# A cross-stage rework of a fused attention and MLP block's schedule: split first load, trickled weight loads, interleaved attention chain

## The chip, the cores and the metric

The kernel runs on one core of one Trainium2 chip. The metric is the device time of one execution in microseconds (us). The kernel before took 895.39 us (median of 4 runs, 894.59 to 896.08). All runs used below are fast unless the text says otherwise.

Ratios are the mean time of one kernel's fast runs over the mean of the fast runs of the kernel before in the same rounds, so they are not quite the ratio of the quoted medians. The kernel before drifted between calls (medians 895.07 to 897.00), so runs of different calls are compared by their ratios.

TensorE is called PE below, VectorE DVE, ScalarE ACT, and the engine that issues the loads SP. A bank is one of the eight parts of `ps`, into which PE writes its results; an eviction is the instruction by which DVE or ACT takes them out. Half clock is a stretch in which the granted clock of PE is 0.5, or, where no clock is recorded, its instructions take about twice their usual time.

## The reference

```python
# S=2048 rows, D=1024, 32 heads of 32, F=3584, bf16
def A(x):                                  # linear attention, x already layernormed
    q, k, v = split(x @ wqkv)              # D -> 3D
    phi = lambda t: where(t > 0, t + 1, exp(t)) + 1e-6
    kv = einsum("bhsd,bhse->bhde", phi(k), v);   z = phi(k).sum over s
    num = phi(q) @ kv;   den = phi(q) @ z + 1e-6
    return (num / den) @ wo
def B(x):                                  # gated MLP
    return (relu(x @ W_gate) * (x @ W_up)) @ W_down
h  = x + A(layernorm(x))
h2 = h + B(layernorm(h))
```

## The kernel before

Rows go in 16 tiles of 128, four of them to a row block of 512. Every instruction is recorded in program order per engine; a small planner turns reads and writes of named buffers (`_Buf`) into semaphore waits. Each engine runs its own list in order. One queue (SP) issues all loads and stores.

The pieces, by the names of the program: `ln1`, `T1` (layernorm and transposes of an x tile), `kvp` (k and v of a tile, 32 matmuls), `kvacc` (adds to kv and z), `kvfin` (masked kv and z to SBUF as `kvm` and `zc`), `a1` (one q unit: 8 matmuls for 128 columns of q over a row block), `a2` (numerator and denominator), `a3` (transposes of o), `a4` (output projection, h, layernorm of h), `a5` (transposes of the normalized h), `g_unit` (gate and up), `d_round` (down).

```python
# loads, in the order in which SP issues them
load_x1(0); load_wkv(0); load_x1(1)
for nt in range(1, NKV): load_wkv(nt)            # 4 chunks of 1 MB in all
for st in range(2, NX1): load_x1(st)             # NX1 = 4 slots for x tiles
for i in range(ND2): load_wq(i)                  # 2 x 1 MB
for i in range(ND2): load_wo(i)                  # 2 x 1 MB
for _ in range(NGS): load_g_next()               # 4 x 1 MB of gate and up weights

ln1(0); ln1(1); T1(0)
for st in range(NST):                            # ln1(st) also issues load_x1(st + 4)
    if st + 1 < NST: T1(st + 1)
    if st + 2 < NST: ln1(st + 2)
    kvp(st)
    if st >= 1: kvacc(st - 1)
kvacc(NST - 1); kvfin()
# ... x2 and W_down loads ...
for (sb_, ct) in a1_units[:26]: a1(sb_, ct, ALL)        # 26 of 32 q units first
for j in range(STB): a2(0, j, ALL)
for j in range(STB):
    if j == STB - 1: filler(ALL)                        # a filler is one of the other 6 q units
    a3(0, j, ALL)
# then a4(0) a4(1) a4(2) a5(0) a4(3) a5(1) f f a5(2) f f a5(3) f
# ...
def a4(r, j, pool):
    ...                                                  # 2 x 8 matmuls, h = . + x
    layernorm(hsb[:, hs, j, :], B_h[hs][j], xn[:, st % 2, :], B_xn[st % 2], "dve", ...)
def a5(r, j, pool):
    (b,) = alloc_banks(pool)
    transpose8(xn[:, st % 2, :], [B_xn[st % 2]], b, NDC, ...)
    ...
# last: d_round: all matmuls of four banks, then four evictions (DVE) and four stores
```

Of the kernel before, what the change touches and what calls it, by code (L numbers as in the profile page):

```python
# [45 lines left out]
class _Plan:  # L46
# [48 lines left out]
    def emit(self, e, eng):  # L95
        seen = {}
        for op in self.prog[e]:
# [15 lines left out]
            ins = op.fn(eng)  # L113
            if last is not None:
                ins._wait_ge(last[0], last[1])
# [6 lines left out]
def bass_sequential_preLN__linear_attn_block__glu_gated_reglu__prompt_kernel(  # L122
# [51 lines left out]
    with es:  # L174
# [89 lines left out]
        sl_x1 = slots("dx1_", NX1)  # L264
        sl_wkv = slots("dwkv_", NKV)
# [11 lines left out]
        B_x1 = bufs("x1_", NX1)  # L277
# [9 lines left out]
        B_kvm = _Buf("kvm")  # L287
        B_zsb = _Buf("zsb")
        B_zc = _Buf("zc")
# [80 lines left out]
        def load_x1(st):  # L370
            i = st % NX1
            dma_load(sl_x1[i], x1[:, i, :], xv[st * P:(st + 1) * P, :], [B_x1[i]], "ld_x1_%d" % st)
# [141 lines left out]
        def ln1(st):  # L514
            i = st % NX1
            layernorm(x1[:, i, :], [B_x1[i]] * NBC, xn[:, st % 2, :], B_xn[st % 2], "dve", "ln1_%d" % st)
            if st + NX1 < NST:
                load_x1(st + NX1)
# [39 lines left out]
        def kvfin():  # L558
            for g in range(NG):
# [3 lines left out]
                       reads=[B_bank[kb], B_bmask], writes=[B_kvm], name="kvm_%d" % g)  # L563
            PL.add("dve", lambda e: e.tensor_copy(out=zsb[:], in_=ps[:, BZ, 0:NG]),
                   reads=[B_bank[BZ]], writes=[B_zsb], name="zsb")
            for g in range(NG):
                PL.add("dve", lambda e, g=g: e.tensor_scalar(out=zc[:, g, :], in0=bmask4[:], scalar1=zsb[:, g:g + 1],
                                                             scalar2=None, op0=ALU.mult),
                       reads=[B_zsb, B_bmask4], writes=[B_zc], name="zc_%d" % g)
# [12 lines left out]
        def a2(r, j, pool):  # L582
# [6 lines left out]
            for g in range(NG):  # L589
# [3 lines left out]
                   True, True, [B_pqT[r][g], B_kvm], B_bank[nbk], "num_%d_%d" % (st, g))  # L593
                mm(ps[:, db, g * HPG:(g + 1) * HPG], pqT[:, r, g, j * P:(j + 1) * P], zc[:, g, :],
                   True, True, [B_pqT[r][g], B_zc], B_bank[db], "den_%d_%d" % (st, g))
# [76 lines left out]
        def d_round(r, dh, banks4):  # L672
# [3 lines left out]
            for ft in range(NFT):  # L676
                c, fl = ft // FTB, ft % FTB
                ws = wd_slot(r, dh, c)
                for j in range(STB):
                    mm(bank(banks4[j], NW), hhT[:, ft, j * P:(j + 1) * P], wdring[:, ws, fl, :],  # L680
                       ft == 0, ft == NFT - 1, [B_hhT[ft], B_wd[ws]], B_bank[banks4[j]],
                       "d_%d_%d_%d" % (r, dh, ft))
                if fl == FTB - 1:
                    load_wd_next()
            for j in range(STB):
# [12 lines left out]
        load_x1(0)  # L698
# [5 lines left out]
        for st in range(2, min(NX1, NST)):  # L704
            load_x1(st)
        for i in range(ND2):
            load_wq(i)
        for i in range(ND2):
            load_wo(i)
        for _ in range(NGS):  # L710
            load_g_next()
# [5 lines left out]
        for st in range(NST):  # L717
            if st + 1 < NST:
                T1(st + 1)
            if st + 2 < NST:  # L720
                ln1(st + 2)
            kvp(st)
# [4 lines left out]

        load_x2(0)
        if NST > 1:
            load_x2(1)  # L730
        for _ in range(NWS):
            load_wd_next()

        ALL = list(range(8))
        a1_units = [(sb_, ct) for sb_ in range(NSB) for ct in range(NG)]
        HB = min(6, max(0, len(a1_units) - NG))
        fillers = a1_units[len(a1_units) - HB:] if HB else []
        for (sb_, ct) in a1_units[:len(a1_units) - HB]:
            a1(sb_, ct, ALL)

        def filler(pool):
            if fillers:
                sb_, ct = fillers.pop(0)
                a1(sb_, ct, pool)

        for j in range(STB):
            a2(0, j, ALL)
        for j in range(STB):
            if j == STB - 1:
                filler(ALL)  # L750
            a3(0, j, ALL)
        seq = []
        for j in range(STB):
            seq.append(("a4", j))
            if j >= 2:
                seq.append(("a5", j - 2))
        for j in range(max(0, STB - 2), STB):
            seq.append(("f", 0))
            seq.append(("f", 0))
            seq.append(("a5", j))  # L760
        seq.append(("f", 0))
        for kind, j in seq:
            if kind == "a4":
                a4(0, j, ALL)
            elif kind == "a5":
                a5(0, j, ALL)
            else:
                filler(ALL)
        while fillers:
            filler(ALL)  # L770
# [4 lines left out]
        for r in range(NSB):  # L775
            bgq = []
            if r + 1 < NSB:
                rn = r + 1
                order = []
                order += [("a2", 0), ("a2", 1), ("a2", 2), ("a3", 0), ("a2", 3), ("a3", 1), ("a4", 0),  # L780
                          ("a3", 2), ("a4", 1), ("a3", 3), ("a5", 0), ("a4", 2), ("a5", 1), ("a4", 3),
                          ("a5", 2), ("nop", 0), ("a5", 3)]
                order = [(k_, j) for (k_, j) in order if j < STB]
                for k_, j in order:
                    bgq.append((k_, rn, j))
            lastpair = None
            for ft in range(NFT):
# [3 lines left out]
                if bgq:  # L791
                    k_, rn, j = bgq.pop(0)
                    if k_ == "a2":
                        a2(rn, j, BG)
                    elif k_ == "a3":
                        a3(rn, j, BG)
                    elif k_ == "a4":
                        a4(rn, j, BG)
                    elif k_ == "a5":
                        a5(rn, j, BG)  # L800
            while bgq:
                k_, rn, j = bgq.pop(0)
                if k_ == "a2":
                    a2(rn, j, BG)
                elif k_ == "a3":
                    a3(rn, j, BG)
                elif k_ == "a4":
# [65 lines left out]
```

## Time and profile before

| what | us |
|---|---|
| span of the profiled run | 894.4 |
| PE busy | 849.3 (95%) |
| PE work in full flow, counted (below) | 844 |
| wait for the fifth x tile, PE | 10.37 |
| q and attention of row block 0 (155.2 to 249.9) | 94.7 |
| end of the last matmul to the end of the span | 4.2 |

The busy table and the rows of 40 slices of the page; a digit is tenths of the slice, PEclk the granted PE clock:

```profile
PE 849.3 (95%) x4521; PEld 409.5 (46%) x4608; DVE 276.4 (31%) x517; ACT 174.4 (20%) x258; POOL 35.1 (4%) x107
PE   5689999997699999999999999999999999999998
PEclk9989999999799999999999999999999999999999
DMA  9911400000014435554244455543235653553052
```

The three weak places of the PE row are the start, the second slice (up to about 45 us) and slices 10 and 11. The rest is full. How full is told by counting: in full flow a 128x512 matmul starts every 0.2158 us. The Trainium skill, "TensorE: Matmul & The Clock Gate", section "Wait — 56ns, not 53.3ns?", gives 215.7 ns, and this trace agrees. The kernel has 3,712 of those, 384 transposes (0.058 us each), 128 k/v plus z pairs (0.080) and 128 numerator plus denominator pairs (0.083): 844 us.

The windows view of the kernel before cuts the span into stages (us of the window, then busy us and number of instructions per engine, the clock, the DMA share and GB/s):

```profile
core 0: us, PE busy (x) PEld busy (x) DVE busy (x) ACT busy (x) POOL busy (x), PEclk, DMA share, GB/s
11.60:36.97 25.37, 24.20 (x143) 11.81 (x143) 7.55 (x16) 9.99 (x15) 2.12 (x6) 1.00 1.10 351
36.97:57.77 20.80, 10.20 (x64) 5.21 (x64) 9.14 (x19) 3.65 (x6) 2.85 (x8) 0.75 0.45 145
155.24:249.93 94.69, 80.76 (x440) 39.93 (x448) 53.16 (x115) 26.15 (x39) 4.24 (x12) 0.93 0.04 12
249.93:890.17 640.24, 636.78 (x3202) 300.17 (x3263) 156.39 (x263) 92.15 (x137) 12.71 (x36) 1.00 0.44 138
```

The MLP (last line, with the attention of blocks 1 to 3 inside) takes what its instructions need. From 11.60 to 36.97 us the DMA is busy throughout: share 1.10, 351 GB/s. The Trainium skill, "DMA: Bandwidth & Descriptors", section "Specifications", gives a limit of about 358 GB/s per core. The rate here is close to it, but it is no hard limit in this case: e8, a run below, moved 370 GB/s from 4 to 8 us. The stretch 36.97 to 57.77 lasts 20.8 us, and its PE work is one step of 8.0 us. Why it takes longer is in the timeline, here of SP (issue of loads; a merged line covers the time from the first of its loads to the last) and then of DVE and PE:

```profile
31.28 2.92 SPq L368 DMA_DIRECT2D gring<-in_B_W_up_dram  x1
34.31 24.86 SPq L368 DMA_DIRECT2D RE<-in_A_x_dram  x7
...
43.99 1.29 DVE L465 BATCH_NORM_STATS2 st<-RE 128x6 f32<-128x512 bf16 x2 [16.43 <-DMA RE<-in_A_x_dram]
47.58 1.01 PE L445 MATMUL ps<-ident,xn 128*128 128x128 bf16 x8 [10.37 <-DVE xn L485]
48.82 8.32 PE L435 MATMUL ps<-RB,RA 128*128 128x512 bf16 x31 [0.23 <-DVE E2t L497]
```

The bracket at the end is the idle time ahead of the instruction and what ended it. The fifth x tile was issued only at 34.31, behind 8 MB of weights that nobody needs before 155 us, and reached DVE at 43.99. PE waited 10.37 us, and then 32 matmuls took 8.3 us instead of 6.9: half clock. The Trainium skill, "TensorE: Matmul & The Clock Gate", section "What's actually happening", says that the clock halves after an idle window of about 3.4 us and comes back after as much work. This trace agrees here: its clock records give half clock from 41.54 to 51.78 us.

Row block 0's layernorms (DVE, writing `xn`) and what PE does around them, from the timeline:

```profile
217.78 0.55 DVE L485 TENSOR_SCALAR xn<-hsb,rstd,nmr 128x1024 bf16<-128x1024 bf16 x1 [1.37 <-POOL nmr L476]
222.32 0.55 DVE L485 TENSOR_SCALAR xn<-hsb,rstd,nmr 128x1024 bf16<-128x1024 bf16 x1 [1.36 <-POOL nmr L476]
226.87 0.55 DVE L485 TENSOR_SCALAR xn<-hsb,rstd,nmr 128x1024 bf16<-128x1024 bf16 x1 [1.37 <-POOL nmr L476]
227.56 1.01 PE L445 MATMUL ps<-ident,xn 128*128 128x128 bf16 x8 [6.40 <-DVE xn L485]
238.25 0.62 PE L445 MATMUL ps<-ident,xn 128*128 128x128 bf16 x8 [4.13 <-DVE xn L485]
249.93 3.62 PE L435 MATMUL ps<-RE,gring 128*128 128x512 bf16 x16
```

PE waits 6.40 and 4.13 us for a layernorm. The last line is the first gate matmul.

The tail, from the timeline: one merged PE line that ends at 890.17, the four evictions, the four stores.

```profile
874.68 15.49 PE L435 MATMUL ps<-wdring,RA 128*128 128x512 bf16 x70
889.62 2.48 DVE L689 TENSOR_TENSOR RC<-ps,hsb 128x512 bf16<-128x512 f32 x4 [21.69 <-PE ps L435]
890.34 2.12 SPq L694 DMA_DIRECT2D out_dram<-RC  x4
```

### The profile page before, as it was taken

To read this page: it belongs to the slowest core of one execution; us is meant where nothing else is said; L and a number is where in the kernel's file an instruction comes from. 1 tells how busy PE (TensorE), PEld (TensorE's weight loads), DVE (VectorE), ACT (ScalarE), POOL (GpSimd) and SP (SyncE) were. 2 spreads that over 40 slices of the span, in tenths; PEclk is the share of its full clock that TensorE was granted. 3 is DMA by queue.
4 is the path that set the end of the run, shared out by engine and by line. 5 is a ranking of instruction groups with operands and counts; after the bars stand their busy time and mean duration, and the time that the engine had idled before them with its cause. 6 is when DMAs were issued, how large, how long until landed. Compare 5 with 4: busy or idle time off the path is not lost.

```text
span 894.4 us, 10887 instructions
## 1 busy us (share of the span) xinstructions
PE 849.3 (95%) x4521; PEld 409.5 (46%) x4608; DVE 276.4 (31%) x517; ACT 174.4 (20%) x258; POOL 35.1 (4%) x107
## 2 busy tenths in 40 slices
PE   5689999997699999999999999999999999999998
PEld 2345555444254444444544444454444444444443
DVE  3155443657343422013434111054321012121111
ACT  3234443331122221000222210022221001111100
POOL 1011110000000000000000000000000000000000
PEclk9989999999799999999999999999999999999999
DMA  9911400000014435554244455543235653553052
GB/s 318 338 37 36 143 1 1 1 1 24 24 42 148 130 107 169 183 165 142 95 137 133 155 172 178 168 142 118 95 119 163 189 187 114 169 164 119 24 175 84
DMA packets 105392, 109.75 MB, mean 123 GB/s; under 512 B 2944, under 2 KB 101248, under 8 KB 105344
## 3 DMA queue, kind: packets, MB, share of 16 engines
q1 hardware_dynamic: 105344, 109.06, 38.5%
q8 instruction: 36, 0.59, 0.3%
q14 instruction: 12, 0.10, 0.0%
HBM read 104.86 MB, written 4.19 MB: 122 GB/s over the span
## 4 chain that ended last, share of the span: by engine, by line
PE 87%; DVE 5%; SPq 4%; ACT 2%; issue 1%; DMA 1%; POOL 1%; DVEq 0%; ACTq 0%
PE ps L435 84%; SPq L368 4%; PE ps L445 3%; DVE RB L500 2%; ACT Et L495 2%; DMA RE<-in_A_x_dram 1%; DVE E2t L497 1%; DVE st L465 1%; DVE hsb L631 0%; POOL rstd L473 0%; DVE RE L606 0%; DVE xn L485 0%; POOL nmr L476 0%; DVE RC L689 0%; DVE kvm L561 0%
## 5 line engine op out<-in xcount | busy, mean ns | idle before, releaser
L435 PE MATMUL ps<-RE,gring 128*128 128x512 bf16 x876 | 196.7, 379 | 1.1
L435 PE MATMUL ps<-RC,gring 128*128 128x512 bf16 x877 | 194.8, 379 | 1.1
L435 PE MATMUL ps<-wdring,RA 128*128 128x512 bf16 x878 | 193.1, 379 | 0.9
L663 DVE TENSOR_TENSOR RA<-RC,ps 128x512 bf16<-128x512 bf16 x112 | 76.9, 687 | 262.1 <-PE ps L435 262.1
L661 ACT ACTIVATE RC<-ps 128x512 bf16<-128x512 f32 x112 | 67.0, 598 | 461.8 <-PE ps L435 461.8
L435 PEld LDWEIGHTS ps<-wdring,RA 128*128 128x128 bf16 x896 | 87.7, 98 | 105.7
L435 PEld LDWEIGHTS ps<-RC,gring 128*128 128x128 bf16 x896 | 87.1, 98 | 102.9
L435 PEld LDWEIGHTS ps<-RE,gring 128*128 128x128 bf16 x896 | 86.3, 98 | 100.1
L435 PE MATMUL ps<-RB,RA 128*128 128x512 bf16 x497 | 112.8, 386 | 1.4 <-DVE E2t L497 0.7
L435 PEld LDWEIGHTS ps<-RB,RA 128*128 128x128 bf16 x512 | 50.1, 99 | 59.4 <-issue 3.9
L689 DVE TENSOR_TENSOR RC<-ps,hsb 128x512 bf16<-128x512 f32 x32 | 19.9, 683 | 178.3 <-PE ps L435 178.3
L435 PE MATMUL ps<-wo,RE 128*128 128x512 bf16 x249 | 59.3, 389 | 0.4
L435 PE MATMUL ps<-RA,RC 128*128 128x512 bf16 x248 | 57.0, 387 | 2.0 <-DVE kvm L561 1.3
L495 ACT ACTIVATE Et<-ps 128x512 bf16<-128x512 f32 x64 | 38.2, 597 | 73.3 <-PE ps L435 30.4
L445 PE MATMUL ps<-ident,xn 128*128 128x128 bf16 x256 | 21.1, 230 | 31.4 <-DVE xn L485 30.7
L435 PEld LDWEIGHTS ps<-wo,RE 128*128 128x128 bf16 x256 | 25.6, 100 | 31.3 <-issue 2.7
L435 PEld LDWEIGHTS ps<-RA,RC 128*128 128x128 bf16 x256 | 25.3, 100 | 31.7 <-issue 2.8
L497 DVE TENSOR_SCALAR E2t<-Et 128x512 bf16<-128x512 bf16 x64 | 18.7, 293 | 65.7 <-ACT Et L495 65.6
L453 ACT ACTIVATE RE<-ps 128x1024 bf16<-128x1024 bf16 x24 | 24.3, 1023 | 56.2 <-PE ps L445 56.2
L445 PEld LDWEIGHTS ps<-ident,xn 128*128 128x128 bf16 x256 | 16.9, 103 | 36.4 <-issue 17.3
L631 DVE TENSOR_TENSOR hsb<-ps,x 128x512 bf16<-128x512 f32 x32 | 21.9, 690 | 32.5 <-PE ps L435 32.5
L470 POOL TENSOR_SCALAR ve<-mv 128x1 f32<-128x1 f32 x32 | 7.1, 223 | 609.4 <-DVE mv L468 609.4
(45 smaller groups left out, 328.9 us busy)
## 6 DMA issues: line engine op xcount, KB each, us to landing
gring<-in_B_W_gate_dram SPq DMA_DIRECT2D x28, 1024.0 KB, 5.3
gring<-in_B_W_up_dram SPq DMA_DIRECT2D x28, 1024.0 KB, 7.3
wdring<-in_B_W_down_dram SPq DMA_DIRECT2D x56, 512.0 KB, 3.6
RE<-in_A_x_dram SPq DMA_DIRECT2D x16, 256.0 KB, 2.8
RB<-in_A_wqkv_dram SPq DMA_DIRECT2D x4, 1024.0 KB, 9.2
x<-in_A_x_dram SPq DMA_DIRECT2D x16, 256.0 KB, 2.6
out_dram<-RC SPq DMA_DIRECT2D x32, 128.0 KB, 3.6
RC<-in_A_wqkv_dram SPq DMA_DIRECT2D x2, 1024.0 KB, 11.2
```

Source lines behind the costliest of these rows:

```text
L368: return PL.add("sp", lambda e: e.dma_start(dst_ap, src_ap), writes=wbufs, slot=slot, name=name)
L435: lambda e: e.matmul(out_ap, lhsT, rhs, start=start, stop=stop, skip_group_check=skip),
L445: lambda e, i=i: e.transpose(tb[:, i, :], src_ap[:, i * P:(i + 1) * P], ident[:]),
L453: PL.add("act", lambda e: e.activation(out=dst_ap, in_=src, func=ACTF.Identity), reads=[B_bank[b]], writes=dst_bufs, name=name)
L465: PL.add("dve", lambda e, c=c: e.bn_stats(out=st6[:, k, c * 6:(c + 1) * 6], in_=src_full[:, c * BCH:(c + 1) * BCH]), reads=[src_chunk_bufs ...
L495: PL.add("act", lambda e: e.activation(out=Et[:, k, 0:w], in_=src, func=ACTF.Exp), reads=[B_bank[b]], writes=[B_E[k]], name=name + "_exp")
L497: PL.add("dve", lambda e: e.tensor_scalar(out=E2t[:, k, 0:w], in0=Et[:, k, 0:w], scalar1=1.0, scalar2=1e-6, op0=ALU.min, op1=ALU.add), rea ...
L500: PL.add("dve", lambda e: e.scalar_tensor_tensor(out=dst_ap, in0=src, scalar=C1, in1=E2t[:, k, 0:w], op0=ALU.add, op1=ALU.max), reads=[B_b ...
L631: PL.add("dve", lambda e, b=b, nt=nt: e.tensor_tensor(out=hsb[:, hs, j, nt * NW:(nt + 1) * NW], in0=bank(b, NW), in1=x2[:, xs, nt * NW:(nt ...
L661: PL.add("act", lambda e: e.activation(out=rg[:, k, :], in_=bank(ga, SBW), func=ACTF.Relu), reads=[B_bank[ga]], writes=[B_rg[k]], name="rg ...
L663: PL.add("dve", lambda e: e.tensor_tensor(out=hhT[:, ft, :], in0=rg[:, k, :], in1=bank(gb, SBW), op=ALU.mult), reads=[B_rg[k], B_bank[gb]] ...
L689: PL.add("dve", lambda e, j=j, k=k: e.tensor_tensor(out=outst[:, k, :], in0=bank(banks4[j], NW), in1=hsb[:, hs, j, dh * NW:(dh + 1) * NW], ...
```

## The change

It keeps every computation and moves them: the first x tile is loaded in two halves; bulk weights are issued a few at a time during the k/v stage; the attention chain of row block 0 starts after its own 8 q units, with the other 24 spread between its pieces; the last output round evicts each bank while the next one's last matmuls run; `kvm` and `zc` get one dependency record per group. (It also attaches names to instructions, which adds none.)

```diff
-        B_kvm = _Buf("kvm")
+        B_kvm = bufs("kvm_", NG)            # the same for zc
...
-        load_x1(0)
+        load_x1(0, split=True)              # two loads of 128 KB on two semaphores
...
-        for i in range(ND2): load_wq(i)     # and wo, gate/up, x2, W_down: all at once
+        bulk = [...]                        # wq, wo, x2(0), x2(1), 4 gate/up, 4 W_down
+        def trickle(n): ...                 # issues the next n of them
...
                 ln1(st + 2)
+            if st >= 1:
+                trickle(2)
             kvp(st)
...
-        # 26 q units, then a2 x4, a3 x4, a4/a5 with 6 fillers (as above)
+        for ct in range(NG):
+            a1(0, ct, ALL)
+        chain = [("a2", 0), ("a2", 1), ("a2", 2), ("a3", 0), ("a2", 3), ("a3", 1), ("a4", 0),
+                 ("a3", 2), ("a4", 1), ("a3", 3), ("a5", 0), ("a4", 2), ("a5", 1), ("a4", 3),
+                 ("a5", 2), ("a5", 3)]
+        # behind each piece: 2 q units (first 8 pieces) or 1 (last 8), from blocks 1 to 3
...
+                if stagger and c == nchunks - 1:     # last round, last 4 of 28 weight tiles
+                    for j in range(STB):
+                        for ft in fts:
+                            d_mm(ft, j)
+                        d_evac(j)
```

More of the change, by code (lines that the diff above doesn't have):

```diff
@@ L113, in emit @@
             ins = op.fn(eng)
+            if op.name:
+                try:
+                    ins.annotate(op.name)
+                except Exception:
+                    pass
             if last is not None:
@@ L264, in bass_sequential_preLN__linear_attn_block__glu_gated_reglu__prompt_kernel @@
         sl_x1 = slots("dx1_", NX1)
+        sl_x1h = slots("dx1h_", NBC)
         sl_wkv = slots("dwkv_", NKV)
@@ L276, in bass_sequential_preLN__linear_attn_block__glu_gated_reglu__prompt_kernel @@
         B_bank = bufs("bank", 8)
-        B_x1 = bufs("x1_", NX1)
+        B_x1 = [bufs("x1_%d_" % i, NBC) for i in range(NX1)]
         B_xn = bufs("xn_", 2)
@@ L286, in bass_sequential_preLN__linear_attn_block__glu_gated_reglu__prompt_kernel @@
         B_E2 = bufs("E2_", 3)
-        B_kvm = _Buf("kvm")
+        B_kvm = bufs("kvm_", NG)
         B_zsb = _Buf("zsb")
-        B_zc = _Buf("zc")
+        B_zc = bufs("zc_", NG)
         B_pqT = [bufs("pqT%d_" % r, NG) for r in range(NSB)]
@@ L368, in dma_load, with load_x1 @@
             return PL.add("sp", lambda e: e.dma_start(dst_ap, src_ap), writes=wbufs, slot=slot, name=name)
-        def load_x1(st):
+        def load_x1(st, split=False):
             i = st % NX1
-            dma_load(sl_x1[i], x1[:, i, :], xv[st * P:(st + 1) * P, :], [B_x1[i]], "ld_x1_%d" % st)
+            if split and NBC > 1:
+                for c in range(NBC):
+                    dma_load(sl_x1h[c], x1[:, i, c * BCH:(c + 1) * BCH], xv[st * P:(st + 1) * P, c * BCH:(c + 1) * BCH],
+                             [B_x1[i][c]], "ld_x1_%d_%d" % (st, c))
+            else:
+                dma_load(sl_x1[i], x1[:, i, :], xv[st * P:(st + 1) * P, :], B_x1[i], "ld_x1_%d" % st)
         def load_wkv(nt):
@@ L515, in ln1 @@
             i = st % NX1
-            layernorm(x1[:, i, :], [B_x1[i]] * NBC, xn[:, st % 2, :], B_xn[st % 2], "dve", "ln1_%d" % st)
+            layernorm(x1[:, i, :], B_x1[i], xn[:, st % 2, :], B_xn[st % 2], "dve", "ln1_%d" % st)
             if st + NX1 < NST:
@@ L562, in kvfin @@
                                                              op=ALU.mult),
-                       reads=[B_bank[kb], B_bmask], writes=[B_kvm], name="kvm_%d" % g)
+                       reads=[B_bank[kb], B_bmask], writes=[B_kvm[g]], name="kvm_%d" % g)
             PL.add("dve", lambda e: e.tensor_copy(out=zsb[:], in_=ps[:, BZ, 0:NG]),
@@ L568, in kvfin @@
                                                              scalar2=None, op0=ALU.mult),
-                       reads=[B_zsb, B_bmask4], writes=[B_zc], name="zc_%d" % g)
+                       reads=[B_zsb, B_bmask4], writes=[B_zc[g]], name="zc_%d" % g)
         def a1(sb_, ct, pool):
@@ L592, in a2 @@
                 mm(ps[:, nbk, (col % 512):(col % 512) + P], pqT[:, r, g, j * P:(j + 1) * P], kvm[:, g, :],
-                   True, True, [B_pqT[r][g], B_kvm], B_bank[nbk], "num_%d_%d" % (st, g))
+                   True, True, [B_pqT[r][g], B_kvm[g]], B_bank[nbk], "num_%d_%d" % (st, g))
                 mm(ps[:, db, g * HPG:(g + 1) * HPG], pqT[:, r, g, j * P:(j + 1) * P], zc[:, g, :],
-                   True, True, [B_pqT[r][g], B_zc], B_bank[db], "den_%d_%d" % (st, g))
+                   True, True, [B_pqT[r][g], B_zc[g]], B_bank[db], "den_%d_%d" % (st, g))
             PL.add("dve", lambda e: e.tensor_scalar(out=dtmp[:, k, :], in0=ps[:, db, 0:H], scalar1=1e-6,
@@ L670, in bass_sequential_preLN__linear_attn_block__glu_gated_reglu__prompt_kernel, with d_round @@
         os_ctr = [0]
-        def d_round(r, dh, banks4):
+        def d_round(r, dh, banks4, stagger=False):
             hs = r % 2
@@ L675, in d_round, with d_mm, d_evac @@
                 touch_bank(b)
-            for ft in range(NFT):
+            def d_mm(ft, j):
                 c, fl = ft // FTB, ft % FTB
                 ws = wd_slot(r, dh, c)
-                for j in range(STB):
-                    mm(bank(banks4[j], NW), hhT[:, ft, j * P:(j + 1) * P], wdring[:, ws, fl, :],
-                       ft == 0, ft == NFT - 1, [B_hhT[ft], B_wd[ws]], B_bank[banks4[j]],
-                       "d_%d_%d_%d" % (r, dh, ft))
-                if fl == FTB - 1:
-                    load_wd_next()
-            for j in range(STB):
+                mm(bank(banks4[j], NW), hhT[:, ft, j * P:(j + 1) * P], wdring[:, ws, fl, :],
+                   ft == 0, ft == NFT - 1, [B_hhT[ft], B_wd[ws]], B_bank[banks4[j]],
+                   "d_%d_%d_%d" % (r, dh, ft))
+            def d_evac(j):
                 st = r * STB + j
@@ L696, in d_round @@
                        reads=[B_outst[k]], slot=sl_out[k], name="st_%d_%d" % (st, dh))
-        load_x1(0)
+            nchunks = NFT // FTB
+            for c in range(nchunks):
+                fts = list(range(c * FTB, (c + 1) * FTB))
+                if stagger and c == nchunks - 1:
[3 more added lines that the diff above has]
+                        d_evac(j)
+                else:
+                    for ft in fts:
+                        for j in range(STB):
+                            d_mm(ft, j)
+                load_wd_next()
+            if not stagger:
+                for j in range(STB):
+                    d_evac(j)
+        load_x1(0, split=True)
         load_wkv(0)
@@ L705, in bass_sequential_preLN__linear_attn_block__glu_gated_reglu__prompt_kernel, with trickle @@
             load_x1(st)
+        bulk = []
         for i in range(ND2):
-            load_wq(i)
+            bulk.append(lambda i=i: load_wq(i))
         for i in range(ND2):
-            load_wo(i)
+            bulk.append(lambda i=i: load_wo(i))
+        bulk.append(lambda: load_x2(0))
+        if NST > 1:
+            bulk.append(lambda: load_x2(1))
         for _ in range(NGS):
-            load_g_next()
+            bulk.append(load_g_next)
+        for _ in range(NWS):
+            bulk.append(load_wd_next)
+        def trickle(n):
+            for _ in range(n):
+                if bulk:
+                    bulk.pop(0)()
         ln1(0)
@@ L726, in bass_sequential_preLN__linear_attn_block__glu_gated_reglu__prompt_kernel @@
         kvfin()
-        load_x2(0)
-        if NST > 1:
-            load_x2(1)
-        for _ in range(NWS):
-            load_wd_next()
-        ALL = list(range(8))
-        a1_units = [(sb_, ct) for sb_ in range(NSB) for ct in range(NG)]
-        HB = min(6, max(0, len(a1_units) - NG))
-        fillers = a1_units[len(a1_units) - HB:] if HB else []
-        for (sb_, ct) in a1_units[:len(a1_units) - HB]:
-            a1(sb_, ct, ALL)
-        def filler(pool):
-            if fillers:
-                sb_, ct = fillers.pop(0)
-                a1(sb_, ct, pool)
@@ L746, in bass_sequential_preLN__linear_attn_block__glu_gated_reglu__prompt_kernel @@
-        for j in range(STB):
-            a2(0, j, ALL)
-        for j in range(STB):
-            if j == STB - 1:
-                filler(ALL)
-            a3(0, j, ALL)
-        seq = []
-        for j in range(STB):
-            seq.append(("a4", j))
-            if j >= 2:
-                seq.append(("a5", j - 2))
-        for j in range(max(0, STB - 2), STB):
-            seq.append(("f", 0))
-            seq.append(("f", 0))
-            seq.append(("a5", j))
-        seq.append(("f", 0))
@@ L762, in bass_sequential_preLN__linear_attn_block__glu_gated_reglu__prompt_kernel @@
-        for kind, j in seq:
-            if kind == "a4":
-                a4(0, j, ALL)
-            elif kind == "a5":
-                a5(0, j, ALL)
-            else:
-                filler(ALL)
-        while fillers:
-            filler(ALL)
+        trickle(len(bulk))
+        ALL = list(range(8))
+        for ct in range(NG):
+            a1(0, ct, ALL)
+        rest = [(sb_, ct) for sb_ in range(1, NSB) for ct in range(NG)]
+        chain = [("a2", 0), ("a2", 1), ("a2", 2), ("a3", 0), ("a2", 3), ("a3", 1), ("a4", 0),
+                 ("a3", 2), ("a4", 1), ("a3", 3), ("a5", 0), ("a4", 2), ("a5", 1), ("a4", 3),
+                 ("a5", 2), ("a5", 3)]
@@ new lines, in bass_sequential_preLN__linear_attn_block__glu_gated_reglu__prompt_kernel, with run_piece @@
+        chain = [(k_, j) for (k_, j) in chain if j < STB]
+        nper = []
+        remaining = len(rest)
+        for i in range(len(chain)):
+            left = len(chain) - i
+            n = (remaining + left - 1) // left
+            nper.append(n)
+            remaining -= n
+        def run_piece(k_, r, j, pool):
+            if k_ == "a2":
+                a2(r, j, pool)
+            elif k_ == "a3":
+                a3(r, j, pool)
+            elif k_ == "a4":
+                a4(r, j, pool)
+            elif k_ == "a5":
+                a5(r, j, pool)
@@ L772, in bass_sequential_preLN__linear_attn_block__glu_gated_reglu__prompt_kernel @@
+        for i, (k_, j) in enumerate(chain):
+            run_piece(k_, 0, j, ALL)
+            for _ in range(nper[i]):
+                if rest:
+                    sb_, ct = rest.pop(0)
+                    a1(sb_, ct, ALL)
+        while rest:
+            sb_, ct = rest.pop(0)
+            a1(sb_, ct, ALL)
         BG = [4, 5, 6, 7]
@@ L777, in bass_sequential_preLN__linear_attn_block__glu_gated_reglu__prompt_kernel @@
             if r + 1 < NSB:
-                rn = r + 1
-                order = []
-                order += [("a2", 0), ("a2", 1), ("a2", 2), ("a3", 0), ("a2", 3), ("a3", 1), ("a4", 0),
-                          ("a3", 2), ("a4", 1), ("a3", 3), ("a5", 0), ("a4", 2), ("a5", 1), ("a4", 3),
-                          ("a5", 2), ("nop", 0), ("a5", 3)]
-                order = [(k_, j) for (k_, j) in order if j < STB]
-                for k_, j in order:
-                    bgq.append((k_, rn, j))
+                order = [("a2", 0), ("a2", 1), ("a2", 2), ("a3", 0), ("a2", 3), ("a3", 1), ("a4", 0),
+                         ("a3", 2), ("a4", 1), ("a3", 3), ("a5", 0), ("a4", 2), ("a5", 1), ("a4", 3),
+                         ("a5", 2), ("nop", 0), ("a5", 3)]
+                bgq = [(k_, r + 1, j) for (k_, j) in order if j < STB]
             lastpair = None
@@ L792, in bass_sequential_preLN__linear_attn_block__glu_gated_reglu__prompt_kernel @@
                     k_, rn, j = bgq.pop(0)
-                    if k_ == "a2":
-                        a2(rn, j, BG)
-                    elif k_ == "a3":
-                        a3(rn, j, BG)
-                    elif k_ == "a4":
-                        a4(rn, j, BG)
-                    elif k_ == "a5":
-                        a5(rn, j, BG)
+                    run_piece(k_, rn, j, BG)
             while bgq:
                 k_, rn, j = bgq.pop(0)
-                if k_ == "a2":
-                    a2(rn, j, BG)
-                elif k_ == "a3":
-                    a3(rn, j, BG)
-                elif k_ == "a4":
-                    a4(rn, j, BG)
-                elif k_ == "a5":
-                    a5(rn, j, BG)
+                run_piece(k_, rn, j, BG)
             other = 1 - lastpair
@@ L813, in bass_sequential_preLN__linear_attn_block__glu_gated_reglu__prompt_kernel @@
             for dh in range(ND2):
-                d_round(r, dh, dsets[dh % 2][:STB] if STB <= 4 else None)
-            off = (other - 0) % 2
+                d_round(r, dh, dsets[dh % 2][:STB], stagger=(r == NSB - 1 and dh == ND2 - 1))
             if ND2 % 2 == 0:
-                pass
+                off = other
             else:
```

## The prediction

> **What bounds it.** TensorE: PE busy 849.3 of 894.4 us (95%, the page's busy table), 87% of the chain of waits. In full flow a 128x512 matmul starts every 0.2158 us (timeline). 3,712 of those (801 us), 384 transposes (0.058), 128 k/v plus z pairs (0.080) and 128 numerator plus denominator pairs (0.083) make 844 us, so about 50 us are PE idle or at half clock. From the first gate matmul (249.9) to the last matmul (889.8) it takes 640 us for a count of 641: nothing to win there. By the timeline the loss is elsewhere:
> - start to the first k/v matmul, 12 us;
> - 36.9 to 47.6: PE idle 10.4 us. The fifth x tile, issued at 34.3 behind 8 MB of wq, wo, gate and up weights (DMA share 1.1), landed at 44.0. Then half clock for 10.2 us. The stretch 36.97 to 57.77 should take 8.0 us: 12.7 lost.
> - 1.26 us before the first q matmul (kvm evictions);
> - q and attention of row block 0, 155.2 to 249.9: 94.7 us for PE work of 75.2 (32 q units of 1.718; a2 0.66, a3 0.46, a4 3.45, a5 0.46, four each). Gaps 1.65+0.98 (bank release), 6.40 and 4.13 (layernorm before the transposes), and half clock after them: 19.5 lost.
> - tail 4.6 us after the last matmul.
>
> **What the change does.**
> 1. Trickle: bulk weights go two at a time from step 1 on, so x tiles 4 to 7 pass ahead of them. Worth nearly all of the 12.7; no new starvation: each x tile is issued four 8 us steps ahead, two bulk loads take about 6 us.
> 2. Interleave: the chain starts after 8 q units, the other 24 go 2 or 1 behind each of its 16 pieces. Layernorm latency (first h eviction to transpose, 4.1 us) is covered by over 9 us for tiles 0 to 2. Left: about 1.1 us at the first a2 (the last phi takes 1.7 us, seven groups cover 0.6), 0.2 us at the last a5, small bubbles. DVE has about 63 us of work in these 75: tight, no limit. I count 2.8 us lost instead of 19.5: gain 16.7. The 1.26 stay.
> 3. Staggered last round: its last eviction ends one eviction behind PE, not three: 1.1 us.
> 4. Split first x load: its layernorm starts a little earlier, but the first k/v matmul waits for x tile 1, behind 1 MB of weights and now one issue (0.37 us) later: loss 0.3.
> 5. Per-group kvm/zc dependencies: nothing, long done when a2 starts.
>
> The Trainium skill, "TensorE: Matmul & The Clock Gate" (Part 1), says the clock halves after about 3.4 us idle and recovers after as much work; this trace agrees (half clock after the 10.4, 6.4 and 4.1 us gaps, in multiples of 3.41 us), so removing gaps pays more than their length.
>
> **Sum:** 895.4 - 12.7 - 16.7 - 1.1 + 0.3 = 865.2 us, range 860 to 872. Faster by over 2% 0.95, within 2% 0.04, slower 0.01.
>
> **Right if:** PE share about 98%; no PE idle over 2 us after the first k/v matmul; no DVE wait for an x tile after 20 us; first q matmul at about 142 us (now 155), first gate matmul at 220 (now 250); half clock only before 20 us and at most one later window; last matmul to end 3.5 us.
>
> **Wrong if:** x tiles still starve behind trickled weights; DVE or ACT backlog (phi, evictions, layernorm, in order) stalls PE in the interleaved stretch by over 3 us; short gaps still trip the half clock; the start shifts by over 0.5 us.

## The result and the profile after

865.04 us (median of 8 runs, 864.80 to 866.09), ratio 0.9659 (95% interval 0.9649 to 0.9668). The prediction was 865.2.

The same stages in the windows view of the changed kernel (one step of k/v, block 0's chain, the MLP, the tail), and the page's first rows:

```profile
PE 842.1 (97%) x4520; PEld 406.5 (47%) x4608; DVE 274.9 (32%) x517; ACT 174.1 (20%) x258; POOL 35.1 (4%) x107
PE   4999999999999999999999999999999999999998
38.40:46.80 8.40, 8.35 (x68) 4.63 (x67) 3.92 (x8) 3.81 (x6) 1.46 (x4) 1.00 0.75 250
143.88:220.77 76.89, 74.88 (x439) 37.32 (x447) 51.52 (x114) 25.94 (x39) 4.24 (x12) 1.00 0.05 14
220.77:861.00 640.23, 636.73 (x3201) 300.18 (x3263) 157.91 (x265) 92.15 (x137) 12.71 (x36) 1.00 0.44 139
861.00:864.00 3.00, 0.02 (x1) 0.00 (x0) 0.69 (x1) 0.00 (x0) 0.00 (x0) 1.00 0.38 128
```

Block 0's chain went from 94.69 to 76.89 us. Of those 17.8 us, 11.9 are idle time (13.93 to 2.01, window less PE busy) and 5.9 are busy time, that is, matmuls no longer at half clock (80.76 to 74.88). The MLP took the same 640.2 us. What is left of waits in the middle, and the start, by the timeline of PE and DVE:

```profile
8.89 1.28 DVE L476 BATCH_NORM_STATS2 st<-RE 128x6 f32<-128x512 bf16 x2 [2.42 <-DMA RE<-in_A_x_dram]
13.22 9.21 PE L446 MATMUL ps<-RB,RA 128*128 128x512 bf16 x32
...
143.88 13.76 PE L446 MATMUL ps<-RA,RC 128*128 128x512 bf16 x62 [0.88 <-DVE kvm L572]
159.43 0.23 PE L446 MATMUL ps<-kvm,RB 128*128 128x128 bf16 x1 [1.25 <-DVE RB L511]
218.60 0.61 PE L456 MATMUL ps<-ident,xn 128*128 128x128 bf16 x8 [0.32 <-DVE xn L496]
220.77 3.62 PE L446 MATMUL ps<-RE,gring 128*128 128x512 bf16 x16
```

The trickle, by the timeline of SP: x tiles 2 to 7 are now issued ahead of the first `wq` chunk, and no wait of DVE for an x tile is left after 20 us.

```profile
8.91 18.79 SPq L374 DMA_DIRECT2D RE<-in_A_x_dram  x6
27.75 1.28 SPq L374 DMA_DIRECT2D RC<-in_A_wqkv_dram  x2
```

The start got worse: x tile 1 reached DVE at 8.89 us (7.32 before), and the first k/v matmul started at 13.22 us (11.64 before). The tail got shorter, three evictions now running ahead of the last matmul's end:

```profile
849.63 11.39 PE L446 MATMUL ps<-wdring,RA 128*128 128x512 bf16 x51
858.52 0.69 DVE L699 TENSOR_TENSOR RC<-ps,hsb 128x512 bf16<-128x512 f32 x1 [19.75 <-PE ps L446]
861.11 0.69 DVE L699 TENSOR_TENSOR RC<-ps,hsb 128x512 bf16<-128x512 f32 x1 [0.17 <-PE ps L446]
```

The account of the spans, 894.4 to 864.0: first q matmul 11.36 us earlier (155.24 to 143.88), chain 17.80 shorter, MLP 0.0, tail 1.2 shorter: 30.4. The sum is the predicted one. The experiments ask whether its parts are right, and for the right reasons.

### The profile page after: what moved, and what is told of

Its sections match the earlier page's. It is cut to its first block, busy times and chain, and to the rows that moved or that the text cites. A ratio compares the mean times of both kernels' runs of the same rounds, so it can differ in the third digit from the quotient of the medians.

```text
span 864.0 us, 10884 instructions
## 1 busy us (share of the span) xinstructions
PE 842.1 (97%) x4520; PEld 406.5 (47%) x4608; DVE 274.9 (32%) x517; ACT 174.1 (20%) x258; POOL 35.1 (4%) x107
## 4 chain that ended last, share of the span: by engine, by line
PE 95%; DVE 2%; DMA 1%; issue 1%; ACT 1%; POOL 0%; SPq 0%; ACTq 0%; DVEq 0%
PE ps L446 93%; PE ps L456 2%; DMA RE<-in_A_x_dram 1%; DVE RB L511 1%; ACT Et L506 1%; DVE E2t L508 0%; DVE st L476 0%; DVE kvm L572 0%; SPq L374 0%; POOL rstd L484 0%; DVE zc L578 0%; DVE xn L496 0%; DVE RC L699 0%; DVE hsb L642 0%; POOL nmr L487 0%
## 5 line engine op out<-in xcount | busy, mean ns | idle before, releaser
L446 PE MATMUL ps<-wo,RE 128*128 128x512 bf16 x250 | 57.5, 379 | 0.3
L547 ACT ACTIVATE RE<-ps 128x512 bf16<-128x512 f32 x32 | 19.1, 597 | 35.4 <-PE ps L446 35.4
```

Source lines behind the costliest of these rows:

```text
L446: lambda e: e.matmul(out_ap, lhsT, rhs, start=start, stop=stop, skip_group_check=skip),
L547: PL.add("act", lambda e, b=b, j=j: e.activation(out=vv[:, slot, j * NW:(j + 1) * NW], in_=bank(b, NW), func=ACTF.Identity), reads=[B_bank ...
```

## The experiments

The two kernels above are compared with these twelve runs, of 4 to 6 timed executions each. In e12 one execution was slow and is left out. The 95% intervals of the ratios are 0.001 to 0.002 wide to each side, 0.9 to 1.8 us. Gains of 12 to 18 us stand far outside them; differences of about 1 us between variants rest on the traces.

| run | what it is | median us | ratio |
|---|---|---|---|
| (changed kernel) | | 865.04 | 0.9659 |
| e1_no_split | changed, first load whole | 864.19 | 0.9647 |
| e4_one_buffer | changed, one record for kvm, one for zc | 865.50 | 0.9662 |
| e5_no_stagger | changed, old last round | 866.35 | 0.9671 |
| e6_six_fillers | changed, six q units in the chain | 868.41 | 0.9691 |
| e2_trickle_only | before, loads trickled | 883.94 | 0.9863 |
| e3_interleave_only | before, q units and chain as changed | 878.39 | 0.9797 |
| e13_own_tile | before, one exchange in the chain | 882.56 | 0.9854 |
| e12_busy_gaps | before, throwaway work in waits | 902.70 | 1.0079 |
| e8_fill | e1 plus middle gaps filled | 861.47 | 0.9610 |
| e9_start | e1 plus reordered start | 862.29 | 0.9623 |
| e10_all | e8 and e9, with clock warm-up | 858.92 | 0.9581 |
| e11_all_busy | e10, warm-up without gaps | 857.74 | 0.9569 |

### The two large parts, each alone

e2 puts only the `bulk` list and `trickle(2)` into the kernel before; e3 puts only the new q order and chain into it (both edits are as in the diff above).

> The kernel before with only the order of the loads changed: bulk weights two at a time from step 1 on. My prediction gives this 12.7 us; with the first x load unsplit there is no shift of the start. So 895.1 minus 12.6, about 882.5 us, and the 10.4 us PE gap at 37 us and its half clock are gone, while the chain of row block 0 keeps its gaps. Rival: the two parts overlap (a faster start is given back in the chain, which waits for loads that now come later): less than 11 us.

> The kernel before with only the q units and the chain of row block 0 reordered as in the change. From the traces of before and after, the stretch from the first q matmul to the first gate matmul should go from 94.7 to about 77 us: 895.1 minus 17.7, about 877.4 us; the 10.4 us gap at 37 us stays. Together with the trickle-only run the two gains should add up to the whole change but for about 1 us (tail plus 1.2, evictions of kvm and zc plus 0.4, split minus 0.9). Rival: they overlap, and the sum of the two gains is more than 2 us above 30.

The ratios 0.9863 and 0.9797 are gains of 12.3 and 18.2 us of the 896.5 us that the kernel before took in these rounds. They sum to 30.5; the whole change has 30.6 by its ratio. So the parts add up within the noise of about 1.5 us, and neither hides the other. In e2's trace the 10.37 us wait is gone while 6.38 and 4.13 us stay in the chain; in e3's trace it is the reverse (10.21 us ahead of the fifth tile, 1.25 and 0.32 in the chain). The trickle term of the prediction (12.7) was right, and so was its size for the chain. Not its reason, as the next two runs show.

### What the chain had waited for

Two runs ask whether it is the spread q units that hide the layernorm. e6 takes 18 of the 24 out of the changed chain again:

```diff
+        for _ in range(len(rest) - 6):
+            sb_, ct = rest.pop(0)
+            a1(sb_, ct, ALL)
...
-            nper.append(n)
-            remaining -= n
+            nper.append(0 if i < len(chain) - 6 else 1)
```

> The changed kernel with the new order of the chain of row block 0, but 18 of its 24 q units put ahead of the chain again; only six, as before the change, stand inside it, one behind each of its last six pieces. Theory A: the order (tiles staggered against each other, so that one tile's layernorm runs under the next tile's matmuls) does most of it, the number of fillers the rest: 865 plus 3 to 6 us, about 869, with gaps of 1 to 3 us at the third a2 and after it. Theory B: the fillers do it: with six, most of the 17.8 us come back and the time is above 877 us.

It took 868.41 us, 3.4 more than the changed kernel by the medians and 2.9 by the ratios. The new order with as few fillers as before keeps about 14.5 of the 17.8 us: its chain lasts 80.2 us (144.04 to 224.22). Its trace has the old bank waits among the a2 pieces (1.65 and 1.13 us), one window of half clock from the second of them on (194.06 to 197.47 us) and no layernorm wait over 0.32 us. Theory A holds, and what the other 18 q units save is the bank waits and the slow matmuls after them, not layernorm latency.

e13 goes the other way. It takes the kernel before, with its 26 q units ahead and six fillers, and makes one exchange:

```diff
         for j in range(STB):
-            seq.append(("a4", j))
             if j >= 2:
                 seq.append(("a5", j - 2))
+            seq.append(("a4", j))
```

> The kernel before with one exchange: in row block 0 the transposes of tile j-2 stand ahead of the output projection of tile j instead of behind it, as they do in the change. The normalized tiles share two slots. In the kernel before, the transposes of tile 0 stand behind the layernorm of tile 2, which overwrites slot 0, so they wait for (and read) tile 2's values; the trace shows them 0.14 us after that layernorm ends, 9.2 us after tile 0's own. Theory: the 6.40 and 4.13 us waits and the half clock behind them are that order's, not a lack of filler; with the exchange TensorE waits about 0.9 and 0.6 us there. Followed by hand with the durations of the trace, the first gate matmul comes at about 236.4 instead of 249.9 us: minus 13.5, a ratio of about 0.985. Rival (my prediction's reading): layernorm latency is what is waited for and needs the spread q units to hide it: then the exchange alone gives less than 5 us.

Measured: ratio 0.9854, 882.56 us, a gain of 13.1 us. The timeline of PE in e13, to be read against the three PE lines of the kernel before:

```profile
218.33 0.62 PE L445 MATMUL ps<-ident,xn 128*128 128x128 bf16 x8 [0.68 <-DVE xn L485]
222.96 0.61 PE L445 MATMUL ps<-ident,xn 128*128 128x128 bf16 x8 [0.56 <-DVE xn L485]
236.38 3.62 PE L435 MATMUL ps<-RE,gring 128*128 128x512 bf16 x15
155.89:236.38 80.49, 75.50 (x440) 37.31 (x447) 52.72 (x115) 26.15 (x39) 4.21 (x12) 1.00 0.05 14
```

The waits of 6.40 and 4.13 us are now 0.68 and 0.56, and the first gate matmul comes at 236.38 us (expected 236.4). The last line, of the windows view, shows the whole stage: 80.49 us instead of 94.69, of which 8.9 are idle time and 5.3 half clock.

So most of the chain's gain, 13 of about 18 us, is that of one exchange. `xn` has two slots, chosen by `st % 2`. In the kernel before, `a5(0)` stands behind `a4(2)` in program order. The planner records dependencies in that order, so `a5(0)` gets the last writer of slot 0, which is tile 2's layernorm. PE waited for tile 2, and it then read tile 2.

That is also an error of data, not only of time: in the kernel before, tiles 0 and 1 of row block 0 get the MLP of tiles 2 and 3. No race check can see it, as every access is ordered, and the comparison with the reference passed in both orders. That the wrong tile is read follows from the program order and the planner's rule; no run looked at these rows alone. Evaluated on the host with and without W_down, the reference's MLP term has a root mean square of 0.00019 against 0.078 for the output; exchanging those two tiles' terms changes the output by at most 0.0015, and by 0.001 in relative norm. The change, which puts `a5(j)` ahead of `a4(j + 2)`, repairs this.

### The small parts

e1 takes the split out of the changed kernel:

```diff
-        load_x1(0, split=True)
+        load_x1(0)
```

> The changed kernel with the first x tile loaded in one piece again. In the changed kernel the first k/v matmul starts at 13.2 us against 11.6 before, because x tile 1 landed at 8.9 us instead of 7.3. Theory: the split causes the whole shift. Then without it x tile 1 lands at about 7.3, the first k/v matmul starts at 11.6 and the kernel takes about 863.4 us (1.6 less than 865.0). Rival: the shift comes from the run (the rate of the DMA in its first microseconds) or from the rest of the change; then the first k/v matmul stays at about 13.2 and the time at 865.0.

Measured: 864.19 us (864.09 to 864.47), no run of it as slow as the fastest of the changed kernel (864.80). The timeline has the times of before again:

```profile
7.55 1.29 DVE L476 BATCH_NORM_STATS2 st<-RE 128x6 f32<-128x512 bf16 x2 [0.60 <-DMA RE<-in_A_x_dram]
11.87 8.79 PE L446 MATMUL ps<-RB,RA 128*128 128x512 bf16 x32
```

In the four traces with the split (changed kernel, e4, e5, e6), x tile 1 reaches DVE at 7.92 to 9.27 us, in the nine others that can be compared at 7.25 to 7.74. The split costs about 0.9 us by the medians and 1.1 by the ratios, less than the expected 1.6: the profiled execution of the changed kernel, from which the 1.6 was read, was itself 0.7 us above the median. The split did what it was meant to (x tile 0 reaches DVE at 3.01 us against 3.64 before), but k/v does not wait for that tile. In the microsecond from 3 to 4 us the loads move 129 to 227 GB/s with the split and 313 to 379 without, and among the four with the split, the lower that rate, the later tile 1. The load of tile 1 is also issued 0.46 us later (2.15 instead of 1.69 us). Whether that and the lower rate make up the whole delay was not settled.

e4 gives all groups of `kvm` and of `zc` one record again:

```diff
-        B_kvm = bufs("kvm_", NG)
-        B_zc = bufs("zc_", NG)
+        B_kvm = [_Buf("kvm")] * NG
+        B_zc = [_Buf("zc")] * NG
```

> The changed kernel with one dependency record for all groups of kvm and one for all of zc, as before the change. Theory: with one record each eviction waits for the semaphore of the one ahead of it on the same engine; the eight kvm evictions go back to 2.56 us (1.67 in the changed kernel), the eight zc to 2.08 (1.15), the gap ahead of the first q matmul from 0.88 to 1.26 us, and the kernel takes 0.4 us longer: 865.4 us. Rival (my prediction): the records are worth nothing, and the shorter gap is a matter of when the evictions start: 865.0, evictions still 1.67.

The time (865.50, ratio interval 0.9645 to 0.9679) does not tell it from the changed kernel; the trace does. The eight evictions of `kvm` and the eight of `zc`, from the timeline of DVE, first in the changed kernel:

```profile
142.71 1.67 DVE L572 TENSOR_TENSOR kvm<-ps,bmask 128x128 bf16<-128x128 f32 x8 [2.70 <-PE ps L446]
144.49 1.15 DVE L578 TENSOR_SCALAR zc<-bmask,zsb 128x4 bf16<-128x4 f32 x8
```

and in e4:

```profile
141.70 2.57 DVE L572 TENSOR_TENSOR kvm<-ps,bmask 128x128 bf16<-128x128 f32 x8 [2.70 <-PE ps L446]
144.38 2.08 DVE L578 TENSOR_SCALAR zc<-bmask,zsb 128x4 bf16<-128x4 f32 x8
```

With one record seven of the eight evictions wait for the one ahead of them: they start 0.325 us apart instead of 0.198, so about 0.13 us each (0.90 over 7). On PE this is 0.38 us at the first q matmul (1.26 before and 0.88 after, both traces seem to lack the record of the first matmul there; 1.03 in e4 against 0.65 in e1 and e5).

e5 gives the last round its old form:

```diff
-                d_round(r, dh, dsets[dh % 2][:STB], stagger=(r == NSB - 1 and dh == ND2 - 1))
+                d_round(r, dh, dsets[dh % 2][:STB], stagger=False)
```

> The changed kernel with the last output round as before: all four evictions after all matmuls. Theory: the tail from the last matmul's end to the end of the span goes from 3.0 back to 4.2 us, 866.2 us in all (plus 1.2). Rival: the stores, not the evictions, end last, and the staggering hides nothing: plus less than 0.4.

866.35 us, 1.3 more than the changed kernel (1.1 by the ratios), and 4.2 us from the end of the last matmul in its trace: as expected.

### Idle time against half clock: a run that failed

e12 was to keep PE busy inside the waits of the kernel before without taking them away:

```diff
+        BUSY = {"T1_4": 165, "T5_2": 95, "T5_3": 58}
...
             tb = bank_bf(b)
+            for _ in range(BUSY.get(name, 0)):
+                PL.add("pe", lambda e: e.transpose(tb[:, 0, :], ident[:], ident[:]),
+                       reads=[B_ident], writes=[B_bank[b]], name="busy")
```

> The kernel before, with throwaway transposes of the identity on TensorE inside three of its waits (165 ahead of the transposes of the fifth x tile, 95 and 58 ahead of the last two layernorm transposes of row block 0), each set a little shorter than the wait. No wait is removed, but TensorE does not fall idle in them. Theory: of the 12.7 and 19.5 us that I charged to the two stretches, 2.0 and about 4 us are the half clock after the waits; with the engine kept busy they go and the waits stay: minus 5 to 6 us, about 890 us, with fewer or no half-clock windows in the two stretches. Rival: the clock has nothing to do with idleness, or the slow matmuls there have another cause: unchanged, within 1 us.

It took 902.70 us, 7.1 more by its ratio, and the design was at fault. It was made before e13, when I still thought that the two waits stood ahead of the last two tiles' transposes. They stand ahead of tiles 0 and 1, so 153 throwaway transposes (8.5 us at 0.056) came on top of work that had no wait. The 165 of the first place write the bank that the real transposes use. That bank may not have been free in the wait, since DVE, which empties banks in order, was itself stuck behind the x tile; no trace of a normal execution of e12 exists to show it. One hint: the five fast executions had a mean granted clock of 0.986 to 0.992, the kernel before in the same rounds 0.983 to 0.987. So there was mostly less half clock, but not where, or what it was worth; the run does not settle the question.

Its profiled execution showed 1,873 us, with PE busy 97% of it.

```profile
PE 1824.4 (97%) x4837; PEld 662.4 (35%) x4926; DVE 278.6 (15%) x517; ACT 174.7 (9%) x258; POOL 35.1 (2%) x107
721.73 17.49 PE L435 MATMUL ps<-RE,gring 128*128 128x512 bf16 x37 [0.28 <-issue]
739.05 5.83 PE L435 MATMUL ps<-wdring,RA 128*128 128x512 bf16 x12
```

37 matmuls from 721.73 to 739.05 are 0.468 us each, over twice the 0.2158 of all other runs, and so from end to end. The recorded clock of 1.0 means nothing here: the trace of this execution holds no clock record, and its page has no PEclk row. Why it was slow is not known. It is used for nothing else.

### A version that beats both

The waits left in the changed kernel were filled. e8: the first q unit takes a bank that the evictions do not read, one q unit goes ahead of the first a2, and two instead of one behind the last a4 and the a5 after it.

```diff
         kvfin()
         trickle(len(bulk))
+        for b in (BK0, BK1, BZ):
+            touch_bank(b)
...
+        nper = [2, 2, 2, 2, 2, 1, 1, 1, 1, 1, 1, 1, 1, 2, 2, 1]
+        sb_, ct = rest.pop(0)
+        a1(sb_, ct, ALL)
```

> The changed kernel without the split, and with the three small gaps of its middle filled: the first q unit takes a bank that the kvm evictions do not read, one q unit of block 1 stands ahead of the first a2, and two instead of one behind the last two layernorms. The gaps in the trace are 0.65, 1.25 and 0.32 us. Theory: they are plain waits, so filling them takes off their sum, 2.2 us: 864.2 to about 862.0. Rival: VectorE is what holds the stretch up (63 us of work in 77), then the waits only move: less than 1 us.

861.47 us. No PE wait of 0.15 us or more is left after 23 us. It gained 2.7 us on e1 by the medians and 3.3 by the ratios, a little more than the 2.2 of the gaps.

e9 reorders the start, so that the k/v matmuls of tile 0 do not stand behind the transposes of tile 1:

```diff
+        load_wkv(1); load_wkv(2); load_x1(2); load_wkv(3); load_x1(3)
...
         T1(0)
+        kvp(0, [0])                 # the first of four weight chunks only
+        T1(1)
+        kvp(0, [1]); kvp(1, [0, 1])
+        ln1(2)
+        kvp(0, [2]); kvp(1, [2]); kvp(0, [3]); kvp(1, [3])
+        T1(2); ln1(3); kvacc(0); trickle(2)
+        # the loop goes on from st = 2
```

> The changed kernel without the split and with only the reordered start (k/v matmuls of tile 0 do not wait for tile 1, two tiles per weight chunk, x tile 2 ahead of the last chunk), no warm-up transposes and the middle as changed. Theory: first k/v matmul at 9.2 instead of 11.9 us, the third tile's matmuls about 2.8 us earlier: 864.2 to about 861.4. Rival: the weight chunks, not the x tile, hold the start (4 MB arrive at about 350 GB/s until 15 us), then the first matmul is earlier but later chunks are waited for: gain under 1.5 us.

862.29 us, ratio 0.9623 against e1's 0.9647: 2.2 us (1.9 by the medians, 1.3 between the profiled spans), less than the expected 2.8. The first k/v matmul started at 9.51 us, and the waits for later weight chunks that the rival expected are not in the trace. Where the rest of the 2.8 went was not settled.

e10 adds e8's edits and 44 transposes of the identity on PE during the first loads, to have the clock up when real work comes. e11 has 52 of them, and 22 more between tile 0's transposes and the first k/v matmul:

```diff
+        for _ in range(52):
+            PL.add("pe", lambda e: e.transpose(bank_bf(7)[:, 0, :], ident[:], ident[:]),
+                   reads=[B_ident], writes=[B_bank[7]], name="warm_pe")
         ln1(0)
         ln1(1)
         T1(0)
+        # 22 more of them, then kvp(0, [0])
```

> The version meant to beat both: the middle gaps filled as in the other run (minus 2.2), the start reordered (k/v matmuls of tile 0 no longer wait for tile 1; tiles 0 and 1 go through each k/v weight chunk together; x tile 2 ahead of the last chunk): first k/v matmul at about 9.2 us instead of 11.9, and no gaps before the third tile, minus 3.4; and 44 transposes of the identity on the idle TensorE from about 1.6 us, so that its clock is at full rate when the k/v matmuls start: minus up to 1.9. Sum: 864.2 to about 856.7 us. If the clock falls back in the short gap after the first transposes, 858.6.

> The combined version with 52 warm-up transposes instead of 44, and 22 more between the first tile's transposes and the first k/v matmul, so that TensorE has no gap over about 0.4 us in which its clock may fall back, as it did for one window of 3.4 us in the combined run (858.9 us). Theory: that window costs half its length, 1.7 us: about 857.2 us and no half-clock window after the first 8 us. Rival: the window length and its phase decide; unchanged at 858.9.

e10 took 858.92 us (expected 858.6 if the clock falls back). In its trace PE was idle 1.42 us ahead of the first k/v matmul and the clock fell back once: the windows view gives 0.73 for 8 to 12 us and 0.84 for 12 to 16. In e11 the 22 transposes filled that wait:

```profile
7.17 0.62 PE L456 MATMUL ps<-ident,xn 128*128 128x128 bf16 x8 [1.02 <-DVE xn L496]
7.62 1.39 PE L761 MATMUL ps<-ident 128*128 128x128 bf16 x22
9.21 1.67 PE L446 MATMUL ps<-RB,RA 128*128 128x512 bf16 x7 [0.19 <-issue]
11.62 12.25 PE L446 MATMUL ps<-RB,RA 128*128 128x512 bf16 x55
```

The first 7 recorded k/v matmuls take 1.67 us, which is full rate, where the changed kernel's first ones ran at half. e11's trace holds no clock record, so full rate is read from these durations alone. The run took 857.74 us (857.60 to 857.86; expected 857.2), ratio 0.9569 to the kernel before and so 0.9907 to the changed kernel (0.9569 over 0.9659).

## Why the prediction was right or wrong, point by point

The time was right to 0.2 us, partly because errors cancelled.

- Trickle, predicted 12.7: right. Alone it gave 12.3 (e2). None of the predicted dangers came: DVE waited for no x tile after 20 us.
- Interleave, predicted 16.7: right in size (17.8 in the trace, 18.2 alone in e3), wrong in its mechanism. The step that failed is "6.40 and 4.13 (layernorm before the transposes)", read as a latency that the q units must cover. PE waited for the layernorm of another tile, two ahead, because of the order over two shared slots. One exchange without any more filler recovers 13.1 us (e13), and the spread fillers are worth about 3 (e6), by way of the bank waits. The sum came out right because I charged every wait of the stretch as recoverable, whatever its cause. The leftover waits, predicted 1.1 and 0.2, were 1.25 and 0.32. DVE, put at 63 us of work, was busy 51.5 us in the chain.
- Stagger, predicted 1.1: right (1.2 in the spans, 1.3 in e5).
- Split, predicted a loss of 0.3: right in sign, mis-sized. Tile 1 came 1.6 us later in the profiled run; the time lost is about 0.9 us (e1). A shift of the start by over 0.5 us was one of the prediction's own signs of being wrong, and it came.
- Per-group records, predicted "nothing, long done when a2 starts": wrong. I looked at who reads `kvm` and not at the writers, which had waited for each other: 0.38 us at the first q matmul (e4).
- Half clock: the claim that removing a gap pays more than its length holds in the chain (11.9 us idle and 5.9 us of slow matmuls, e13 8.9 and 5.3). At the fifth x tile "Then half clock for 10.2 us" is misread: 6.0 of those 10.2 us lay in the wait itself. That keeping PE busy alone would also remove the slow part was tried at the start only (e10 against e11); in the waits of the kernel before it was not settled, as e12 was misplaced.
- Landmarks: first q matmul 143.9 (predicted 142; the start is most of the difference), first gate matmul 220.8 (220), tail 3.4 when it is counted from the start of the last matmul, as the prediction did (3.5), PE share 97% (98%).

## What to carry to other kernels

When an engine waits for a buffer that is one of a few rotating slots, ask which tenant of the slot it waits for: a reader placed behind the next writer in program order waits too long and reads the wrong tile, race-free, and a tolerance can hide it. On one in-order load queue, issue what the next steps need ahead of what a later stage needs, even where the sum of bytes is the same. And when a prediction agrees to a fraction of a per cent, still run its parts alone: here two of five terms were off, the largest was right in size for a wrong reason, and the sum still came out.

## What the Trainium skill lacked or had wrong

- "VectorE: DVE Perf Modes", section "The DRAIN you can't avoid", says of eight copies with a semaphore after each that "the semaphore costs nothing extra here". Those copies take 13.88 us in all, and whether each waits for the one ahead is not told. Here eight short evictions that wait for one another's semaphore take 2.57 us and those that do not 1.67: 0.13 us for each of seven waits. The sentence does not carry over to short instructions that wait.
- "TensorE: Matmul & The Clock Gate", section "What's actually happening", gives an idle window of about 3.4 us as what halves the clock. Further down the page tells, without a duration, of short idles between banks that make the clock oscillate. In the kernel before, a half-clock window of 3.4 us came after waits of 1.65 and 0.98 us (granted clock 0.53 from 206 to 209 us), and in e6 one began in the second of two waits of 1.65 and 1.13; in e13 waits of 1.65, 0.98 and 0.74 us at the same place left it at 1.00; in e10 waits of 0.92 and 1.42 us were followed by such a window. Shorter waits can do it, and not in every run.
- The same page, section "Seeing it yourself", warns that clock records can be unreliable. It does not say that they can be missing, and that the views then show full clock: in the first 14.2 us of the kernel before, where eight transposes take 1.01 us instead of 0.61, and in the whole of e12's profiled execution (0.468 us per 128x512 matmul, 1,873 us in all).
- "DMA: Bandwidth & Descriptors" has lower rates for smaller loads, but no page that I read tells what splitting the first of several loads on one queue does to those behind it: x tile 1, two loads further on, reached its reader at 7.92 to 9.27 us instead of 7.25 to 7.74.
